# A spectral layer with routed experts: the cast of Y behind the next X on ScalarE, the gate products behind bias and first-stage copy on VectorE

## The chip, the core and the metric

One core of a Trainium2 chip runs the kernel. The metric is device time in microseconds of one execution. TensorE (PE) does the matmuls, VectorE (DVE) and ScalarE (ACT) empty PSUM and do elementwise work, POOL (GpSimd) does elementwise work on SBUF only and two indirect DMAs per expert batch, SyncE (SP) issues the other DMAs.

## The reference

Eight sequences of 3136 rows and 256 columns go through a Fourier layer and then through one expert that takes 128 rows of each:

```python
X = np.fft.rfft(x, axis=1)
Yr = Xr @ w_r - Xi @ w_i + b_r
Yi = Xr @ w_i + Xi @ w_r + b_i
Y = sign(Y) * np.maximum(np.abs(Y) - 0.01, 0)      # both parts
x = np.fft.irfft(Y, n=3136, axis=1)
scores = np.einsum('bsd,d->bs', x, w_gate)
top = the 128 rows of the largest scores of each sequence
out[b, top] = x[b, top] + sigmoid(scores[b, top]) * (relu(x[b, top] @ w1) @ w2)
```

## The kernel before

3136 is 49 times 64, so the transform runs in two stages of matmuls with tables. `s1` is the first stage (49 points); it writes A to DRAM. `s2` reads A back (tile `av`), multiplies by the table `g_sb` into the PSUM tile `px`, and makes X. `spectral` multiplies X by the two weight matrices into `py`. `shrink_a` and `shrink_b` add the bias and apply the soft threshold, which gives Y. `s2i` and `s1i` are the inverse stages: `s2i` makes C (PSUM tile `s`, copied to `ct`, stored to DRAM), `s1i` reads C back (`cv`) and writes the output.

Products are exact to fp32 by pairs: each operand is a rounded part (`Xh`, `Yh`) and the rest (`Xl`, `Yl`), and `mm3` (L200 to L203) issues three matmuls for one. The elementwise work of a step is this. For X: ScalarE casts px to Xh (L429) and a negated half of it (L430), VectorE subtracts for the rest Xl (L431), POOL negates a part of Xl (L432). For Y: VectorE adds the bias in PSUM (L453), ScalarE makes r (L455), VectorE makes yf (L460), ScalarE casts yf to Yh (L462), POOL subtracts for Yl (L463). For C: ScalarE copies it to `ct` (L481), VectorE multiplies it by the gate vector and sums, in two instructions `junk` with a short read of the sum after each (L484): the gate pair.

Work is cut into steps of one group g (13 to a sequence; 12 of two slices and one, g = 12, of one slice) for 8 sequences, 104 steps. Step t issues, in this order: loads and stores; `s2` of step t+1; the first half of `spectral` of t; `s2i` of t-2 with its gate pair; the second half of `spectral`; `shrink_a` of t; `s1` of a sequence 20 steps ahead (8 in 13 steps), whose result ScalarE and VectorE copy by halves (L406, L407); `shrink_b` of t; `s1i` of a unit 32 steps back (8 in 13 steps), whose result ScalarE copies twice (`ot`, L518). Between these, `threads` advance the routing (scores, a search for the threshold by bits, positions; small VectorE operations and small matmuls into the PSUM tile `m`) and the expert's products.

From step 8 on `ordered` chains what these functions issue, so that PE, ScalarE, VectorE and SP keep the order in which the code issues it; POOL's order, and the place of what is not chained (routing, constants such as the casts `w2h` of the W2 slices, L193), is left to a scheduler. `px` has one PSUM buffer, `py` two, `s` four, `m` one; X and yf have two buffers each, Y three, r one.

Of the kernel before, what the change touches and what calls it, by code (L numbers as in the profile page):

```python
# [10 lines left out]
F32 = mybir.dt.float32  # L11
# [6 lines left out]
ALU = mybir.AluOpType  # L18

B, S, D = 8, 3136, 256  # L20
# [76 lines left out]
def fourier_moe(ctx: ExitStack, tc: tile.TileContext, x, w_r, w_i, b_r, b_i, wg, w1, w2,  # L97
                t_wf, t_wq, t_g, t_gi, t_m, t_dig, outs, cap):
    nc = tc.nc
# [3 lines left out]
    pool = ctx.enter_context(tc.tile_pool(name="work", bufs=2))  # L103
# [5 lines left out]
    As, Cs, xt, ct, av, cv, ot, X, Y, Csc, py, r1 = [{} for _ in range(12)]  # L109

    def c_tile(shape, dt, name):
        return const.tile(shape, dt, name=name)
# [13 lines left out]
    wgb = c_tile([128, D], F32, "wgb")  # L126
# [69 lines left out]
    def pair(h_shape, tag, bufs):  # L196
        return (pool.tile(h_shape, F32R, name=tag + "h", bufs=bufs),
                pool.tile(h_shape, F32R, name=tag + "l", bufs=bufs))

    def mm3(out, wh, wl, mh, ml, start=True, stop=True):  # L200
        nc.tensor.matmul(out, wh, mh, start=start, stop=False)  # L201
        nc.tensor.matmul(out, wl, mh, start=False, stop=False)  # L202
        return nc.tensor.matmul(out, wh, ml, start=False, stop=stop).ins  # L203
# [167 lines left out]
    def width(g):  # L371
        return 1 if g == G - 1 else 2
# [3 lines left out]
    def store(dst, src):  # L376
        if t < 0:
            nc.sync.dma_start(out=dst, in_=src)
        else:
            stores.append((dst, src))  # L380
# [76 lines left out]
    def shrink_b(b, g):  # L457
        w = width(g)
        yf = pool.tile([128, w, D], F32, name="yf")
        nc.vector.scalar_tensor_tensor(out=yf, in0=py.pop((b, g)), scalar=0.0, in1=r1.pop((b, g)), op0=ALU.min, op1=ALU.add)  # L460
        yh, yl = pair([128, w, D], "Y", YB)
        nc.scalar.copy(out=yh, in_=yf)  # L462
        nc.gpsimd.tensor_tensor(out=yl, in0=yf, in1=yh.bitcast(F32), op=ALU.subtract)  # L463
        Y[b, g] = yh, yl

    def s2i(b, g):
        w = width(g)
        if g == 0:
            Cs[b] = As[b]
            Csc[b] = pool.tile([128, NJ], F32, name="Csc")  # L470
            nc.vector.memset(Csc[b][:, NJ - 1:], 0.0)
        if g % 2 == 0:
            ct[b] = pool.tile([128, 4, D], F32, name="ct")
        yh, yl = Y.pop((b, g))
        r = 128 if w == 2 else 64
        p = ps.tile([r, w, D], F32, name="s", bufs=4)
        for q in range(w):
            main_pe[0] = mm3(p[:, q, :], gih[:, 2 * g + q, :r], gil[:, 2 * g + q, :r], yh[:, q, :], yl[:, q, :])
        o = 2 * (g % 2)
        c = ct[b][:r, o:o + w, :]  # L480
        nc.scalar.copy(out=c, in_=p)  # L481
        for k in range(w):
            junk = pool.tile([128, D], F32, name="junk", bufs=1)
            nc.vector.tensor_tensor_reduce(out=junk[:r], in0=c[:, k, :], in1=wgb[:r], scale=1.0, scalar=0.0,  # L484
                                           op0=ALU.mult, op1=ALU.add, accum_out=Csc[b][:r, 2 * g + k:2 * g + k + 1])
        if w == 1:
            store(Cs[b][:, N1 - 1].rearrange("h n d -> n h d"), ct[b][:r, o, :].rearrange("p (h d) -> p h d", h=2))
        elif g % 2 == 1:
            for h in range(2):
                store(Cs[b][h, 4 * g - 4:4 * g + 4].rearrange("(j q) n d -> (q n) j d", q=2), ct[b][:, :, 128 * h:128 * h + 128])  # L490

    def score(b):
        p = ps.tile([NJ, 128], F32, name="m", bufs=1)
# [28 lines left out]
    G, U, ORD = 13, 8, 8  # L522
# [54 lines left out]
    def tick(ts):  # L577
        for g in list(ts):
            if g is urgent:
                with tc.high_priority():  # L580
                    end = next(g, 0) == 0
            else:
                end = next(g, 0) == 0
            if end:
                ts.remove(g)
# [3 lines left out]
    def ordered(f, *args, engines=()):  # L589
        bb = nc.cur_bb.bb.instructions  # L590
        n = len(bb)
        f(*args)
        for i in bb[n:]:
            if i.engine in (engines or (PE, ACT, DVE, SP)):
                if i.engine in chain:
                    tc.add_manual_dep(i, chain[i.engine].name, mybir.DependencyInfo(
                        mybir.DependencyClass.NoSync, mybir.DependencyReason.DATA), reason="main order")
                chain[i.engine] = i

    def at_step(u, f, n, kind=None):  # L600
        if 0 <= u < B * G:
            for i in range(-(-(u * n) // G), -(-((u + 1) * n) // G)):
                if t < ORD:
                    f(*divmod(i, n))
                else:
                    ordered(f, *divmod(i, n))
                if kind and i % n == n - 1:
                    done[kind] = i // n
# [19 lines left out]
    for t in range(-LEAD, B * G):  # L628
        if t + LEAD < G:
            at_step(t + LEAD, s1, U)  # L630
        if t == -2:
            consts_g(1)
            consts_gi(0)
        at_step(t + AP, ld_a, G)
        for i in range(U):
            if t == -3 + i * 8 // U:
                ld_x(1, i)
        if t + LEAD + XP >= 2 * G:
            at_step(t + LEAD + XP, ld_x, U)
        to_step(t + 2, ld_c)  # L640
        if t < ORD:
            flush()
        else:
            ordered(flush)
        if t % 2 == 0 and (t + 4) // 2 in range(2, 7):
            consts_g((t + 4) // 2)
        if t % 2 and (t + 1) // 2 in range(0, 6):
            consts_gi((t + 1) // 2 + 1)
        if t == 10:
            consts_b()  # L650
        if t in range(20, 20 + 2 * (FF // 128 + 2), 2):
            consts_moe((t - 20) // 2)
        at_step(t + 1, s2, G)
        tick(threads)
        at_step(t, lambda b, g: spectral(b, g, 0), G)
        if t == B * G - 1:
            at_step(t, shrink_a, G)
            at_step(t, shrink_b, G)
        at_step(t - 2, s2i, G, "s2i")
        if t == B * G - 1:  # L660
            break
        at_step(t, lambda b, g: spectral(b, g, 1), G)
        at_step(t, shrink_a, G)
        for i in range(U):
            if t == i * 8 // U:
                s1(1, i)
        if t + LEAD >= 2 * G:
            at_step(t + LEAD, s1, U)
        at_step(t, shrink_b, G)
        if t < B * G - 2:  # L670
            to_step(t, s1i)
        tick(threads)
        if main_pe[0] is not None:
            with tc.issue_after(main_pe[0]):
                ticks[0] += 1
                tick(ffns)
# [27 lines left out]
    unit()  # L704
    fill(0)
    unit()
    ordered(s2i, B - 1, G - 2)
    ordered(s2i, B - 1, G - 1)
    done["s2i"] = B - 1
    ordered(flush)  # L710
    stored = True
# [41 lines left out]
```

## Time and profile before

| | |
|---|---|
| median of 3 runs | 741.06 us (740.42 to 743.32) |
| the profiled execution | 740.18 us, its span 738.4 us |
| PE busy | 685.0 us, 93% of the span |
| weight loads busy | 556.9 us, 75% |
| VectorE busy | 455.2 us, 62% |
| ScalarE busy | 378.6 us, 51% |
| POOL busy | 223.8 us, 30% |
| DMA moved | 195.29 MB, mean 264 GB/s |
| share of the last chain | PE 46%, VectorE 21%, ScalarE 13%, DMA 9% |

Busy is the time in which an engine has an instruction under way. The ends of matmuls are modelled: a matmul is listed as longer than the distance to the next. An idle time is shown with what ended it. All groups of rows below come from the profiled execution.

### The profile page before, as it was taken

What the parts mean: (1) busy time and instruction counts of PE and PEld (TensorE: products, weight loads), DVE (VectorE), ACT (ScalarE), POOL (GpSimd) and SP (SyncE); (2) the same over time, 40 slices, a digit from 0 to 9 for tenths busy, and PEclk for the clock granted to TensorE, in tenths of its full rate; (3) what the DMA queues carried; (4) which work ended last, traced back from release to release, by engine and by line L of the source; (5) the groups of instructions that cost most, each with busy time, mean ns of one, the idle gap of its engine ahead of it and who ended that gap; (6) DMA issues with size and microseconds to landing.
All of it is one profiled execution on the core that took longest, in us unless ns stands there. A gap on an engine that the chain in (4) does not pass through costs nothing.

```text
span 738.4 us, 15016 instructions
## 1 busy us (share of the span) xinstructions
PE 685.0 (93%) x5482; PEld 556.9 (75%) x5482; DVE 455.2 (62%) x1330; ACT 378.6 (51%) x759; POOL 223.8 (30%) x255
## 2 busy tenths in 40 slices
PE   6299999999999999999999999999899999988997
PEld 2188787988877778887888787777778887865666
DVE  3146566565545555555677667777786758876752
ACT  3045545555555555656555655555555445445441
POOL 0043333233333332223233333322322322223221
PEclk9589999999999999999999999999999999999999
DMA  8888987787888899989999998897567765656961
GB/s 318 307 287 287 342 273 217 240 260 221 249 282 273 271 320 323 304 293 340 320 301 300 329 302 279 306 305 257 192 200 230 237 190 172 215 175 212 363 245 40
DMA packets 146407, 195.29 MB, mean 264 GB/s; under 512 B 8453, under 2 KB 111262, under 8 KB 146334
## 3 DMA queue, kind: packets, MB, share of 16 engines
q1 hardware_dynamic: 145278, 192.10, 78.3%
q0 software_dynamic: 912, 2.21, 0.9%
q8 instruction: 43, 0.70, 0.4%
q14 instruction: 30, 0.25, 0.1%
q10 hardware_dynamic: 144, 0.03, 0.0%
HBM read 100.58 MB, written 93.85 MB: 263 GB/s over the span
## 4 chain that ended last, share of the span: by engine, by line
PE 46%; DVE 21%; ACT 13%; DMA 9%; issue 8%; SPq 1%; POOL 1%; DVEq 0%; POOLq 0%; ACTq 0%
PE s L391 10%; PE px L426 7%; PE py L201 6%; PE py L203 6%; PE py L202 6%; DVE yf L460 4%; DVE junk L484 4%; ACT r L455 4%; DVE py L453 4%; ACT ot L518 3%; DVE Xl L431 3%; DMA xe<-in_moe_w 3%; ACT Xh L429 2%; PE s L203 2%; PE s L201 2%
## 5 line engine op out<-in xcount | busy, mean ns | idle before, releaser
L463 POOL TENSOR_TENSOR Yl<-yf,Yh 128x512 fp32r<-128x512 f32 (+1 forms) x104 | 133.5, 1284 | 314.5 <-ACT Yh L462 314.5
L455 ACT ACTIVATE r<-py,m2l 128x512 f32<-128x512 f32 (+1 forms) x104 | 69.9, 672 | 192.8 <-DVE py L453 178.3
L431 DVE TENSOR_TENSOR Xl<-px,Xh 128x512 fp32r<-128x512 f32 (+1 forms) x104 | 69.7, 670 | 150.3 <-ACT Xh L430 128.3
L426 PEld LDWEIGHTS px<-g_sb,av 128*128 128x128 f32 (+1 forms) x800 | 99.2, 194 | 67.0 <-DVE Csc L484 18.7
L426 PE MATMUL px<-g_sb,av 128*128 128x128 f32 (+1 forms) x800 | 117.6, 289 | 25.0 <-DMA av<-As 14.6
L201 PE MATMUL py<-wrh,Xh 128*128 128x256 f32 x400 | 122.8, 307 | 0.0
L202 PE MATMUL py<-wrh,Xl 128*128 128x256 f32 x400 | 112.9, 282 | 0.0
L203 PE MATMUL py<-wrl,Xh 128*128 128x256 f32 x400 | 112.8, 282 | 0.0
L201 PE MATMUL py<-wih,Xh 128*128 128x256 f32 x400 | 112.7, 282 | 0.0
L202 PE MATMUL py<-wih,Xl 128*128 128x256 f32 x400 | 112.2, 281 | 0.0
L203 PE MATMUL py<-wil,Xh 128*128 128x256 f32 x400 | 112.2, 280 | 0.0
L460 DVE SCALAR_TENSOR_TENSOR yf<-py,r 128x512 f32<-128x512 f32 (+1 forms) x104 | 69.7, 670 | 51.0 <-ACT r L455 50.0
L484 DVE CUSTOM_DVE_ANT_0 junk<-ct,wgb 128x256 f32<-128x256 f32 (+1 forms) x200 | 92.0, 460 | 14.1 <-ACT ct L481 10.8
L462 ACT CAST Yh<-yf 128x512 fp32r<-128x512 f32 (+1 forms) x104 | 62.8, 603 | 57.3 <-DVE yf L460 56.9
L432 POOL TENSOR_SCALAR Xl<-Xl 128x256 fp32r<-128x256 f32 (+1 forms) x104 | 50.2, 482 | 113.7 <-DVE Xl L431 86.8
L201 PEld LDWEIGHTS py<-wrh,Xh 128*128 128x128 f32 x400 | 76.5, 191 | 2.7 <-issue 1.4
L391 PE MATMUL s<-xt,w1f 49*64 49x512 f32 x480 | 70.6, 646 | 6.7 <-DMA w1f<-t_wf 5.0
L202 PEld LDWEIGHTS py<-wrh,Xl 128*128 128x128 f32 x400 | 76.5, 191 | 0.0
L203 PEld LDWEIGHTS py<-wil,Xh 128*128 128x128 f32 x400 | 75.6, 189 | 1.1 <-issue 1.1
L203 PEld LDWEIGHTS py<-wrl,Xh 128*128 128x128 f32 x400 | 76.2, 190 | 0.0
L201 PEld LDWEIGHTS py<-wih,Xh 128*128 128x128 f32 x400 | 75.8, 190 | 0.3 <-issue 0.3
L202 PEld LDWEIGHTS py<-wih,Xl 128*128 128x128 f32 x400 | 75.6, 189 | 0.2 <-POOL Xl L432 0.2
(125 smaller groups left out, 1210.7 us busy)
## 6 DMA issues: line engine op xcount, KB each, us to landing
xt<-in_x SPq DMA_DIRECT2D x60, 512.0 KB, 5.1
As<-at SPq DMA_DIRECT2D x59, 512.0 KB, 4.0
cv<-As SPq DMA_DIRECT2D x58, 512.0 KB, 5.6
out<-ot SPq DMA_DIRECT2D x57, 512.0 KB, 3.1
av<-As SPq DMA_DIRECT2D x96, 256.0 KB, 5.1
As<-ct SPq DMA_DIRECT2D x96, 256.0 KB, 4.5
out<-at SPq DMA_DIRECT2D x7, 512.0 KB, 2.7
xt<-As SPq DMA_DIRECT2D x6, 512.0 KB, 10.2
```

The costliest lines, as they stand in the source:

```text
L201: nc.tensor.matmul(out, wh, mh, start=start, stop=False)
L202: nc.tensor.matmul(out, wl, mh, start=False, stop=False)
L203: return nc.tensor.matmul(out, wh, ml, start=False, stop=stop).ins
L391: last_mm = nc.tensor.matmul(out[r][64 * c:64 * c + 64], w[64 * r:64 * r + N1, :], src(r, c), start=True, stop=True)
L426: nc.tensor.matmul(px[:, 2 * p + h, :], a[:, h, 2 * (g % 2) * (w - 1) + p, :], g_sb[:r, 2 * g + p, :], start=True, stop=True)
L431: nc.vector.tensor_tensor(out=xl[:, :, NF:], in0=px, in1=xh[:, :, NF:].bitcast(F32), op=ALU.subtract)
L432: nc.gpsimd.tensor_scalar(out=xl[:, :, :NF], in0=xl[:, :, 2 * NF:].bitcast(F32), scalar1=-1.0, scalar2=1.0, op0=ALU.mult, op1=ALU.mult)
L455: nc.scalar.activation(out=r1[b, g], in_=p, func=AF.Relu, bias=m2l, scale=1.0)
L460: nc.vector.scalar_tensor_tensor(out=yf, in0=py.pop((b, g)), scalar=0.0, in1=r1.pop((b, g)), op0=ALU.min, op1=ALU.add)
L462: nc.scalar.copy(out=yh, in_=yf)
L463: nc.gpsimd.tensor_tensor(out=yl, in0=yf, in1=yh.bitcast(F32), op=ALU.subtract)
L484: nc.vector.tensor_tensor_reduce(out=junk[:r], in0=c[:, k, :], in1=wgb[:r], scale=1.0, scalar=0.0, op0=ALU.mult, op1=ALU.add, accum_out=Cs ...
```

## The change

`shrink_b` is cut in two. What makes yf stays; the cast to Yh and POOL's subtraction become `shrink_c`, issued a step later, behind `s2` of the next step. The gate pair leaves `s2i` and becomes `gate`, issued behind `shrink_a` and `s1` and ahead of `shrink_b`.

```diff
--- before.py
+++ after.py
@@ -458,6 +458,11 @@
         w = width(g)
         yf = pool.tile([128, w, D], F32, name="yf")
         nc.vector.scalar_tensor_tensor(out=yf, in0=py.pop((b, g)), scalar=0.0, in1=r1.pop((b, g)), op0=ALU.min, op1=ALU.add)
+        Y[b, g] = yf
+
+    def shrink_c(b, g):
+        w = width(g)
+        yf = Y[b, g]
         yh, yl = pair([128, w, D], "Y", YB)
         nc.scalar.copy(out=yh, in_=yf)
         nc.gpsimd.tensor_tensor(out=yl, in0=yf, in1=yh.bitcast(F32), op=ALU.subtract)
@@ -479,15 +484,20 @@
         o = 2 * (g % 2)
         c = ct[b][:r, o:o + w, :]
         nc.scalar.copy(out=c, in_=p)
-        for k in range(w):
-            junk = pool.tile([128, D], F32, name="junk", bufs=1)
-            nc.vector.tensor_tensor_reduce(out=junk[:r], in0=c[:, k, :], in1=wgb[:r], scale=1.0, scalar=0.0,
-                                           op0=ALU.mult, op1=ALU.add, accum_out=Csc[b][:r, 2 * g + k:2 * g + k + 1])
         if w == 1:
             store(Cs[b][:, N1 - 1].rearrange("h n d -> n h d"), ct[b][:r, o, :].rearrange("p (h d) -> p h d", h=2))
         elif g % 2 == 1:
             for h in range(2):
                 store(Cs[b][h, 4 * g - 4:4 * g + 4].rearrange("(j q) n d -> (q n) j d", q=2), ct[b][:, :, 128 * h:128 * h + 128])
+
+    def gate(b, g):
+        w = width(g)
+        r = 128 if w == 2 else 64
+        c = ct[b][:r, 2 * (g % 2):2 * (g % 2) + w, :]
+        for k in range(w):
+            junk = pool.tile([128, D], F32, name="junk", bufs=1)
+            nc.vector.tensor_tensor_reduce(out=junk[:r], in0=c[:, k, :], in1=wgb[:r], scale=1.0, scalar=0.0,
+                                           op0=ALU.mult, op1=ALU.add, accum_out=Csc[b][:r, 2 * g + k:2 * g + k + 1])
 
     def score(b):
         p = ps.tile([NJ, 128], F32, name="m", bufs=1)
@@ -651,13 +661,16 @@
         if t in range(20, 20 + 2 * (FF // 128 + 2), 2):
             consts_moe((t - 20) // 2)
         at_step(t + 1, s2, G)
+        at_step(t - 1, shrink_c, G)
         tick(threads)
         at_step(t, lambda b, g: spectral(b, g, 0), G)
         if t == B * G - 1:
             at_step(t, shrink_a, G)
             at_step(t, shrink_b, G)
-        at_step(t - 2, s2i, G, "s2i")
+            at_step(t, shrink_c, G)
+        at_step(t - 2, s2i, G)
         if t == B * G - 1:
+            at_step(t - 2, gate, G, "s2i")
             break
         at_step(t, lambda b, g: spectral(b, g, 1), G)
         at_step(t, shrink_a, G)
@@ -666,6 +679,7 @@
                 s1(1, i)
         if t + LEAD >= 2 * G:
             at_step(t + LEAD, s1, U)
+        at_step(t - 2, gate, G, "s2i")
         at_step(t, shrink_b, G)
         if t < B * G - 2:
             to_step(t, s1i)
@@ -704,8 +718,9 @@
     unit()
     fill(0)
     unit()
-    ordered(s2i, B - 1, G - 2)
-    ordered(s2i, B - 1, G - 1)
+    for g in (G - 2, G - 1):
+        ordered(s2i, B - 1, g)
+        ordered(gate, B - 1, g)
     done["s2i"] = B - 1
     ordered(flush)
     stored = True
```

What this does to the order is seen on ScalarE around the last cast of a W2 slice (`w2h`). A row is a source line, an operation, what it writes and reads, and its size. Before:

```order
L455 ACTIVATE r_2974<-py,m2l 128x256
L193 CAST w2h<-xe 128x256
L406 COPY at<-s 128x512
L462 CAST Yh<-yf 128x256
L518 COPY ot<-s 128x4x128 x2
L429 CAST Xh<-px 128x4x128
L430 ACTIVATE Xh<-px 128x4x64
L481 COPY ct<-s 128x512
L455 ACTIVATE r_3055<-py,m2l 128x512
L462 CAST Yh<-yf 128x512
L429 CAST Xh<-px 128x4x128
```

After:

```order
L455 ACTIVATE r_2970<-py,m2l 128x256
L406 COPY at<-s 128x512
L193 CAST w2h<-xe 128x256
L528 COPY ot<-s 128x4x128 x2
L429 CAST Xh<-px 128x4x128
L430 ACTIVATE Xh<-px 128x4x64
L467 CAST Yh<-yf 128x256
L486 COPY ct<-s 128x512
L455 ACTIVATE r_3051<-py,m2l 128x512
L429 CAST Xh<-px 128x4x128
L430 ACTIVATE Xh<-px 128x4x64
```

The cast of Y stood ahead of the output copies and of both casts of X; it stands behind them, ahead of the copy of C. The first-stage copy (`at`) has changed places with the W2 cast.

On VectorE, a step of one slice in the first sequence with the step ahead of it. Before:

```order
L431 TENSOR_TENSOR Xl<-px,Xh 128x4x128
L484 ISA junk,Csc<-ct,wgb 128x256
L484 ISA Csc 128x1
L484 ISA junk,Csc<-ct,wgb 128x256
L484 ISA Csc 128x1
L453 TENSOR_TENSOR py<-py,bias 128x256
L407 COPY at<-s 128x512
L460 SCALAR_TENSOR_TENSOR yf<-py,r_1142 128x256
L431 TENSOR_TENSOR Xl<-px,Xh 128x4x128
```

After:

```order
L431 TENSOR_TENSOR Xl<-px,Xh 128x4x128
L453 TENSOR_TENSOR py<-py,bias 128x256
L407 COPY at<-s 128x512
L499 ISA junk,Csc<-ct,wgb 128x256
L499 ISA Csc 128x1
L499 ISA junk,Csc<-ct,wgb 128x256
L499 ISA Csc 128x1
L460 SCALAR_TENSOR_TENSOR yf<-py,r_1138 128x256
L431 TENSOR_TENSOR Xl<-px,Xh 128x4x128
```

The four instructions of the gate pair stood between Xl and the bias; they stand behind the bias and the first-stage copy and ahead of yf.

On POOL, in the steps that follow, with the numbers of the tiles (counted in the order in which the program makes them). Before:

```order
L463 TENSOR_TENSOR Yl_1038<-yf_1035,Yh_1037 128x512
L432 TENSOR_SCALAR Xl_1048<-Xl_1048 128x2x64
L463 TENSOR_TENSOR Yl_1096<-yf_1093,Yh_1095 128x512
L432 TENSOR_SCALAR Xl_1110<-Xl_1110 128x4x64
L463 TENSOR_TENSOR Yl_1156<-yf_1153,Yh_1155 128x256
L432 TENSOR_SCALAR Xl_1168<-Xl_1168 128x4x64
```

After:

```order
L432 TENSOR_SCALAR Xl_1044<-Xl_1044 128x2x64
L468 TENSOR_TENSOR Yl_1050<-yf_1035,Yh_1049 128x512
L468 TENSOR_TENSOR Yl_1112<-yf_1093,Yh_1111 128x512
L432 TENSOR_SCALAR Xl_1106<-Xl_1106 128x4x64
L468 TENSOR_TENSOR Yl_1170<-yf_1153,Yh_1169 128x256
L432 TENSOR_SCALAR Xl_1164<-Xl_1164 128x4x64
```

In the narrow step (the row of 128x2x64) Yl and the negation have changed places; otherwise Yl stays ahead of the negation of a part of Xl. In the new program this Xl is the older tile of the two: it is made first and negated second.

## Rows read from the trace of the kernel before

**Rows 1.** The page of the profile: busy us, share of the span, instructions.

```profile
PE 685.0 (93%) x5482; PEld 556.9 (75%) x5482; DVE 455.2 (62%) x1330; ACT 378.6 (51%) x759; POOL 223.8 (30%) x255
```

**Rows 2.** Table of stretches of 100 us: busy us of each engine (instructions), clock, DMA share, GB/s.

```profile
100.00:200.00 100.00, 96.59 (x800) 84.05 (x799) 60.52 (x149) 54.40 (x112) 34.92 (x41) 1.00 0.76 236
300.00:400.00 100.00, 99.90 (x829) 81.54 (x825) 61.89 (x158) 59.72 (x120) 30.19 (x34) 1.00 0.93 311
```

**Rows 3.** PE's waits: what waited, for whom, us in total, times, longest.

```profile
PE px L426 <- DVE Xl L431: 9.6, 11, 1.6
```

**Rows 4.** The same table for the weight loads.

```profile
PEld px L426 <- DVE Xl L431: 16.8, 18, 2.2
```

**Rows 5.** Timeline, 108 to 114 us, PE, VectorE, ScalarE, POOL: start, duration, [idle before].

```profile
108.28 1.16 PE L426 MATMUL px<-g_sb,av 128*128 128x128 f32 x8
113.84 1.16 PE L426 MATMUL px<-g_sb,av 128*128 128x128 f32 x8 [1.29 <-DVE Xl L431]
...
108.22 0.70 DVE L484 CUSTOM_DVE_ANT_0 junk<-ct,wgb 128x256 f32<-128x256 f32 x1
109.31 0.69 DVE L453 TENSOR_TENSOR py<-py,bias 128x512 f32<-128x512 f32 x1
110.89 0.69 DVE L460 SCALAR_TENSOR_TENSOR yf<-py,r 128x512 f32<-128x512 f32 x1 [0.89 <-ACT r L455]
113.09 0.69 DVE L431 TENSOR_TENSOR Xl<-px,Xh 128x512 fp32r<-128x512 f32 x1 [1.51 <-ACT Xh L430]
...
110.10 0.69 ACT L455 ACTIVATE r<-py,m2l 128x512 f32<-128x512 f32 x1 [1.91 <-DVE py L453]
111.61 0.62 ACT L462 CAST Yh<-yf 128x512 fp32r<-128x512 f32 x1 [0.83 <-DVE yf L460]
112.14 0.58 ACT L429 CAST Xh<-px 128x512 fp32r<-128x512 f32 x1
...
112.31 1.27 POOL L463 TENSOR_TENSOR Yl<-yf,Yh 128x512 fp32r<-128x512 f32 x1 [3.24 <-ACT Yh L462]
113.87 0.51 POOL L432 TENSOR_SCALAR Xl<-Xl 128x256 fp32r<-128x256 f32 x1 [0.29 <-DVE Xl L431]
```

**Rows 6.** Timeline around two casts of W2 slices, ScalarE and PE.

```profile
183.60 0.41 ACT L193 CAST w2h<-xe 128x256 fp32r<-128x256 f32 x1 [2.44 <-DMA xe<-in_moe_w]
...
181.51 1.16 PE L426 MATMUL px<-g_sb,av 128*128 128x128 f32 x8 [1.27 <-DVE Xl L431]
186.96 1.16 PE L426 MATMUL px<-g_sb,av 128*128 128x128 f32 x8 [0.75 <-DVE Xl L431]
...
261.19 0.41 ACT L193 CAST w2h<-xe 128x256 fp32r<-128x256 f32 x1 [1.46 <-DMA xe<-in_moe_w]
261.50 0.58 ACT L406 COPY at<-s 128x512 f32<-128x512 f32 x1
262.28 1.08 ACT L518 COPY ot<-s 128x512 f32<-128x512 f32 x2
...
264.97 1.16 PE L426 MATMUL px<-g_sb,av 128*128 128x128 f32 x8 [1.58 <-DVE Xl L431]
```

**Rows 7.** Timeline, PE, three matmuls in a row at 311 us.

```profile
310.97 0.28 PE L202 MATMUL py<-wih,Xl 128*128 128x256 f32 x1
311.09 0.27 PE L203 MATMUL py<-wil,Xh 128*128 128x256 f32 x1
311.47 1.16 PE L426 MATMUL px<-g_sb,av 128*128 128x128 f32 x8
```

**Rows 8.** Timeline at 92 us, VectorE and POOL.

```profile
92.11 1.29 DVE L484 CUSTOM_DVE_ANT_0 junk<-ct,wgb 128x256 f32<-128x256 f32 x1 [0.73 <-ACT ct L481]
...
91.83 1.29 POOL L171 TENSOR_TENSOR gip<-gi,gip 128x512 fp32r<-128x512 f32 x1
```

**Rows 9.** Timeline, PE, first and last wait for the routing's small results.

```profile
504.65 0.43 PE L501 MATMUL m<-sct,wq 25*64 25x32 f32 x8 [0.57 <-DVE d L258]
...
667.26 0.63 PE L306 MATMUL m<-row,hot 128*128 128x34 f32 x4 [0.71 <-DVE row L292]
```

## Prediction, written before the changed kernel was run

> **What bounds the kernel now.** I read the busy table first: TensorE (PE) is busy for 685.0 of 738.4 us [rows 1]. The table by stretches says where the rest lies: between 300 and 400 us PE is busy for 99.9 of 100 us, between 100 and 200 us for 96.6, at full granted clock in both [rows 2]. So in the middle the only thing to be won is what PE waits for. The table of waits names it: eleven times, 9.6 us together, the first matmul on a group of A (px, L426) waited for VectorE's rest of X (Xl, L431), because px has one PSUM buffer and Xl is its last reader [rows 3]. The weight loads show the same wait 18 times, 16.8 us [rows 4].
>
> The timeline of one such step shows why Xl is late [rows 5]. px starts at 108.28 and takes 1.16, so X could be cast from 109.44. But VectorE first runs the gate pair of an older C (108.22 to 109.31), then the bias (109.31), which ScalarE's r follows at 110.10, yf at 110.89, the cast of Y at 111.61, and only then the cast of X at 112.14; Xl starts at 113.09 and the next px at 113.84, 1.29 late. The chain is gate, bias, r, yf, Yh, Xh, Xl. Two of its links have nothing to do with X: the gate pair and Yh.
>
> **The change part by part.** No instruction is added or dropped; ScalarE, VectorE and POOL do the same work.
>
> *Gate behind bias and first-stage copy.* The pair leaves the stretch before the bias. In the step of [rows 5] the bias can then start when its last spectral matmul ends, about 108.4 (px followed at 108.28), not 109.31. r comes 0.79 later, as now, at 109.2, and is done about 0.65 later. The pair, at 1.09 us [rows 5], runs while r runs, 109.0 to 110.1; yf follows, 110.1 to 110.7. So yf comes 0.8 earlier. Cover: where a first-stage copy stands between too, r is hidden by that copy already and yf moves up less, by about 0.3; those steps also have some 1 us more of PE work.
>
> *Y's cast behind X.* Xh now waits only for r and its own px: 109.85 instead of 112.14. From Xh to Xl is 0.95 and from Xl to the next px 0.75 [rows 5]: Xl at 110.8, px possible at 111.55. PE itself is ready at 113.84 - 1.29 = 112.55. So 1.0 us of cover is left, and the wait goes. What is late next is PE itself.
>
> *What is put off.* Yh goes from 111.61 to about 110.8 here (its yf came earlier); in steps with output copies, where it used to precede two copies and Xh, it gets some 1.5 us later. POOL's rest of Y follows it 0.70 later and takes 1.27 [rows 5]; s2i wants it only a whole step on, behind the next px and half a spectral product. At zero, for that. The gate's sums are wanted once per sequence, after its last step. SP's order differs in one place only, the load of a W2 slice against a store of C; at zero. PE's order differs only in where the small matmuls of the routing stand.
>
> *The sum.* What PE really lost is more than the 9.6. The recorded end of a matmul lies 0.27 behind its start while the next starts 0.12 later [rows 7], so a wait of up to 0.15 shows no idle time and a longer one looks 0.15 too short: 311.09 to 311.47 is 0.38, of which 0.26 is lost, and 0.11 of it at most is recorded as idle. With 18 waits of the weight loads: 9.6 + 18 x 0.16 = 12.5. Bounds: 9.6 from [rows 3], 16.8 from [rows 4] (a weight load's wait also counts time in which earlier matmuls still run). I take 12.5, nearer the matmuls' own rows.
>
> Not all of it goes. At 183.60 and at 261.19 ScalarE waited 2.44 and 1.46 us for a W2 slice from DMA, in front of the casts [rows 6]. At the second, the order after has the first-stage copy ahead of that cast and Y's cast behind X, so the 0.78 from 261.50 to 262.28 goes of the wait of 1.58 at 264.97; 0.8 stays. At the first, Xh follows the slice directly, without r, a copy and Y's cast between; but PE arrives earlier by the 1.27 won at 181.51. The wait of 0.75 at 186.96 could go or more than stay; I let 0.7 stay. Together 1.5.
>
> 12.5 - 1.5 = 11.0 us. The profiled execution took 740.2 us (1.8 outside its span): 729.2. The median of the runs shown is 0.9 higher, so I forecast **730.0 us**. The routing stretch, 504 to 668 us, I leave unchanged: PE waits there 15 times, 11.2 us in all, for small VectorE results, the first and the last in [rows 9]. The pair now stands between bias and yf, where VectorE idles 0.89 for r in steps without a copy [rows 5]; that hides nearly all of it. But the small operations are reordered, which may give or take 3 us.
>
> *A port.* At 92.11 a gate product took 1.29 us beside a POOL operation that ran from 91.83 to 93.12, and ended 0.28 after it [rows 8]; in [rows 5] the whole pair takes 1.09. So it stood still. POOL's Yl is moved here, so what it meets counts. From the times above it runs 111.5 to 112.8 and the next pair starts, behind the next bias, after 113: they miss each other by little. By the rows the sum stays. The Trainium skill, SBUF — State Buffer, section Who interferes with whom, says that a VectorE instruction with two SBUF inputs and a POOL instruction that reads SBUF exclude each other, the loser standing fully still; [rows 8] agree for the VectorE side, and that POOL stands still too no row here shows. By that rule the sum would be the same where they miss and is the third rival where they meet.
>
> **The rivals.**
> *Late weights* (chance 0.09). If ScalarE's waits for the W2 slices do not move up as PE does, they swallow what is won between 175 and 265 us: seven waits, the first and the last in [rows 6], 6.0 us, and 0.16 each hidden, 1.1. Left are 12.5 - 7.1 = 5.4: 734.8, as median 735.7. For it: the two casts of [rows 6], DMA 0.93 busy from 300 to 400 us [rows 2]. Against: these loads are issued behind stores of C and A which also come earlier.
>
> *The waits change owner* (0.07). Xl now stands behind the pair and yf. If the pair takes 1.0 longer than 1.09 the cover of 1.0 is gone and Xl is as late as PE's own work allows or later; with as much again the old waits are back: 740. Against: from 111.55 to 112.55 there is room.
>
> *The rest of X pays* (0.06, slower). POOL runs Yl ahead of the quarter of Xl that it negates (L432), and Yl now starts behind X's cast. In the step of [rows 5]: Yh 110.8, Yl 111.5 to 112.8, the negation to 113.3 (0.51). Half a spectral product needs it at 112.55 + 1.1 + 6 x 0.12 = 114.35; the cover is 1.05 us. If Yl and the negation slide by more than that, every one of 104 steps pays: at 0.11 us a step the gain is used up, at 0.2 it is 20.8 - 11.0 = 9.8 slower, 751. For it: the port, which the pair and POOL share; against: the pair, about 1.09 long [rows 5], lies behind a bias that waits for PE, when POOL is done.
>
> That the change does not do what it says is excluded by the order of instructions: Yh stands behind both casts of X, the pair behind the bias, from the eighth step to the last.
>
> **How the numbers follow.** My forecast has 0.78; its own range is 725.5 to 733.5, from 16.8 in place of 12.5 at one end, or 3 us of routing either way. Late weights lie above that, so the range goes to 738; the owner's and the slower case, 0.13, are left out. 0.5% (3.7 us, about what a measurement of this kernel can tell from no change) puts the borders at 737.4 and 744.8. Faster: 0.78 and 0.09, less a little, 0.86; same 0.08; slower 0.06.
>
> **What would show it.** In the profile after, ScalarE should cast X right after r (and the copies that precede it) with no stop for yf, and PE's waits for Xl should fall from 9.6 to about 1.5 us, those left near the W2 slices; PE's busy time stays near 685; VectorE's bias starts with the end of a spectral product in the short steps, and Xl ends at least 0.5 us ahead of the next px. I am wrong if waits of spectral matmuls (L202, L203) for POOL's part of Xl appear, if the routing's 11.2 us grow by more than 3, or if the waits for Xl are gone and the span is not shorter by some 10 us.

## The result: 716.9 us, and the profile after

The changed kernel takes **716.92 us** (median of 4 runs, 714.71 to 720.31) against 742.19 us of the kernel before in the same session (4 runs, 740.42 to 744.11): a ratio of 0.967, 95% interval 0.9638 to 0.9701. It is faster, by 25 us; the forecast was faster by 11, and the range (725.5 to 738) ended above it. The profiled execution after took 720.31 us with a span of 718.5, 19.9 us under the 738.4 of before. It is the slowest of its four, for a reason that the second half of this section shows.

The busy row of the page, and two stretches of 100 us, with the columns of [rows 1] and [rows 2]:

```profile
PE 678.8 (94%) x5482; PEld 556.6 (77%) x5482; DVE 467.2 (65%) x1330; ACT 383.5 (53%) x759; POOL 210.1 (29%) x255
```

```profile
100.00:200.00 100.00, 99.79 (x833) 87.58 (x832) 61.95 (x154) 57.94 (x116) 33.73 (x44) 1.00 0.81 253
300.00:400.00 100.00, 100.00 (x846) 83.45 (x845) 68.06 (x174) 61.94 (x124) 29.54 (x37) 1.00 0.95 320
```

PE has nearly the work of before, 678.8 for 685.0 us. Between 100 and 200 us it is now busy for 99.8 of 100 us, before for 96.6. Where it stood still has shrunk. PE's waits and then the weight loads' waits (what waited, for whom, us in total, times, longest), the rows that answer to [rows 3] and [rows 4]:

```profile
PE px L426 <- DVE Xl L431: 1.0, 2, 0.8
```

```profile
PEld px L426 <- DVE Xl L431: 3.0, 3, 1.6
PEld s L391 <- ACT ct L486: 2.8, 3, 1.6
```

The waits of px for the rest of X fell from 9.6 to 1.0 us. The forecast was about 1.5, left near the W2 slices; of the 1.0, 0.8 lies at 89.9 us, ahead of the first slice, so the size was met by luck. The last row is one whose counterpart I had not weighed. In the same table of the kernel before it reads:

```profile
PEld s L391 <- ACT ct L481: 9.0, 18, 1.7
```

The first stage (s, L391) needs a PSUM buffer that ScalarE's copy of C (ct) must free, and that copy stands behind Xh in ScalarE's order. So what made X late made ct late.

The step that the prediction worked through (108.28 to 113.84 in [rows 5]) now looks like this, in the timeline of PE, VectorE and ScalarE (start, duration, engine, [idle before]):

```profile
105.42 1.05 PE L426 MATMUL px<-g_sb,av 128*128 128x128 f32 x8
105.62 0.70 DVE L453 TENSOR_TENSOR py<-py,bias 128x512 f32<-128x512 f32 x1 [1.94 <-PE py L203]
...
106.23 0.41 DVE L499 CUSTOM_DVE_ANT_0 junk<-ct,wgb 128x256 f32<-128x256 f32 x1
...
106.42 0.69 ACT L455 ACTIVATE r<-py,m2l 128x512 f32<-128x512 f32 x1 [1.63 <-DVE py L453]
...
107.00 0.58 ACT L429 CAST Xh<-px 128x512 fp32r<-128x512 f32 x1
...
107.21 0.69 DVE L460 SCALAR_TENSOR_TENSOR yf<-py,r 128x512 f32<-128x512 f32 x1
...
107.93 0.62 ACT L467 CAST Yh<-yf 128x512 fp32r<-128x512 f32 x1
107.95 0.69 DVE L431 TENSOR_TENSOR Xl<-px,Xh 128x512 fp32r<-128x512 f32 x1
...
108.62 0.58 ACT L486 COPY ct<-s 128x512 f32<-128x512 f32 x1
...
109.53 1.16 PE L426 MATMUL px<-g_sb,av 128*128 128x128 f32 x8
```

From px to px it is 109.53 - 105.42 = 4.11 us, for 5.56 before. The links went as worked out: ScalarE casts X at 107.00, straight behind r, and Yh waits for yf and stands behind; the pair runs beside r; the rest of X ends at 108.64, 0.9 us ahead of px.

To see where the 19.9 us came from I paired the matmuls of the two traces one by one and compared, pair by pair, the distance from one start to the next. That also counts what is hidden in overlapping ends. Gains, in us, of the kernel after on the kernel before:

| stretch (times of before) | at px (L426) | at s (L391) | elsewhere | sum |
|---|---|---|---|---|
| 0 to 38 | -1.1 | 2.4 | 0 | 1.3 |
| 38 to 503, without 245 to 251 | 14.2 | 5.2 | 0.3 | 19.7 |
| 245 to 251 | -0.7 | -2.1 | -2.4 | -5.2 |
| 503 to 668, routing | 0.9 | 0 | 2.5 | 3.4 |
| 668 to the end | 0 | 0.7 | 0.1 | 0.8 |

So from 38 to 503 us the waits of px were worth 14.2 and the first stage's waits for ct 5.2; the routing gave 3.4, and at one place 5.2 was lost. The 1.3 at the start belongs to this execution: in the profiles of after_again and w2_later below it is -0.5. The place of the loss lies at 234 to 246 us in the time of the kernel after. The timeline of ScalarE and of PE, and the table by stretches, show:

```profile
234.82 0.40 ACT L193 CAST w2h<-xe 128x256 fp32r<-128x256 f32 x1 [4.00 <-DMA xe<-in_moe_w]
```

```profile
238.02 1.42 PE L391 MATMUL s<-cv,w1tf 49*64 49x512 f32 x4 [0.69 <-ACT ct L486]
```

```profile
235.00:239.00 4.00, 3.31 (x17) 0.78 (x16) 1.94 (x4) 3.51 (x8) 2.17 (x3) 0.95 0.50 166
239.00:246.00 7.00, 7.00 (x33) 6.41 (x32) 1.94 (x6) 3.23 (x8) 1.73 (x3) 0.54 0.97 311
246.00:252.00 6.00, 6.00 (x53) 4.63 (x52) 4.59 (x12) 4.41 (x10) 2.06 (x3) 1.00 0.99 321
```

ScalarE stood 4.00 us in front of a W2 slice that had not landed; ct behind it came late; PE stood still for 0.69 us at s; and from 239 to 246 us, PE being busy all the time, the granted clock is 0.54 in the mean. From the means of the stretches it was 0.50 (1.2 GHz) from about 238.6 to 245.4. The rows count 33 matmuls in these 7.00 us and 53 in the 6.00 us behind them. Without this loss the profiled execution would have taken some 715 us, which is where two of the other three runs lie.

### The profile page after: what moved, and what is told of

The parts are those of the page before. It is cut to its first block, busy times and chain, and to the rows that moved or that the text cites. A ratio compares the mean times of both kernels' runs of the same rounds, so it can differ in the third digit from the quotient of the medians.

```text
span 718.5 us, 15022 instructions
## 1 busy us (share of the span) xinstructions
PE 678.8 (94%) x5482; PEld 556.6 (77%) x5482; DVE 467.2 (65%) x1330; ACT 383.5 (53%) x759; POOL 210.1 (29%) x255
## 4 chain that ended last, share of the span: by engine, by line
PE 78%; DVE 10%; DMA 5%; issue 3%; ACT 2%; SPq 1%; POOL 0%; POOLq 0%; DVEq 0%; ACTq 0%
PE s L391 16%; PE py L201 12%; PE px L426 12%; PE py L203 11%; PE py L202 11%; PE s L201 3%; PE s L203 3%; PE s L202 3%; PE py L345 2%; DMA As<-ot 1%; DVE junk L499 1%; DVE yf L460 1%; PE s L345 1%; DVE py L453 1%; DVE Xl L431 1%
## 5 line engine op out<-in xcount | busy, mean ns | idle before, releaser
L468 POOL TENSOR_TENSOR Yl<-yf,Yh 128x512 fp32r<-128x512 f32 (+1 forms) x104 | 130.4, 1254 | 349.1 <-ACT Yh L467 349.0
L426 PEld LDWEIGHTS px<-g_sb,av 128*128 128x128 f32 (+1 forms) x800 | 99.7, 194 | 54.6 <-DVE py L453 17.9
L453 DVE TENSOR_TENSOR py<-py,bias 128x512 f32<-128x512 f32 (+1 forms) x104 | 70.3, 676 | 99.3 <-PE py L203 95.8
L426 PE MATMUL px<-g_sb,av 128*128 128x128 f32 (+1 forms) x800 | 116.1, 287 | 16.2 <-DMA av<-As 15.2
L499 DVE CUSTOM_DVE_ANT_0 junk<-ct,wgb 128x256 f32<-128x256 f32 (+1 forms) x200 | 87.3, 437 | 9.2 <-ACT ct L486 6.0
L486 ACT COPY ct<-s 128x512 f32<-128x512 f32 (+1 forms) x104 | 59.3, 572 | 54.8 <-PE s L203 53.5
L391 PE MATMUL s<-xt,w1f 49*64 49x512 f32 x480 | 71.3, 646 | 5.5 <-DMA w1f<-t_wf 5.1
L429 ACT CAST Xh<-px 128x512 fp32r<-128x512 f32 (+1 forms) x104 | 59.5, 572 | 31.7 <-PE px L426 24.7
```

The costliest lines, as they stand in the source:

```text
L391: last_mm = nc.tensor.matmul(out[r][64 * c:64 * c + 64], w[64 * r:64 * r + N1, :], src(r, c), start=True, stop=True)
L426: nc.tensor.matmul(px[:, 2 * p + h, :], a[:, h, 2 * (g % 2) * (w - 1) + p, :], g_sb[:r, 2 * g + p, :], start=True, stop=True)
L429: nc.scalar.copy(out=xh[:, :, NF:], in_=px)
L453: nc.vector.tensor_tensor(out=p, in0=p, in1=bias[:, :w, :], op=ALU.add)
```

## The experiments

Each was timed on one chip together with the kernel before. "Ratio" is to that, with its 95% interval. Edits are against the kernel after unless the kernel before is named, and "..." marks lines left out. The table also has the length of the two shortest steps of the kernel after, number 14 (the one of the prediction) and number 27, from px to px in the timeline:

| kernel | step 14 | step 27 | median us | ratio |
|---|---|---|---|---|
| before | 5.56 | 5.55 | 742 | 1 |
| y_only | 5.05 | 5.32 | 738.45 | 0.9955 (0.9936 to 0.9973) |
| gate_only | 4.73 | 4.73 | 731.11 | 0.9855 (0.9829 to 0.9881) |
| y_ct | 4.11 | 4.11 | 725.53 | 0.9773 (0.9725 to 0.982) |
| after_again | 4.11 | 4.10 | 716.83 | 0.9666 (0.9636 to 0.9695) |
| after_ct | 4.11 | 4.11 | 718.27 | 0.9662 (0.9613 to 0.9711) |
| pair_twice | 4.11 | 4.24 | 726.69 | 0.9786 (0.9738 to 0.9835) |
| before_twice | 6.48 | 6.48 | 814.92 | 1.0974 (1.0933 to 1.1015) |
| px_two | 5.72 | 5.70 | 742.23 | 1.0006 (0.9978 to 1.0034) |
| w2_later | 4.11 | 4.11 | 715.81 | 0.9645 (0.9619 to 0.967) |
| w2_ct | 4.11 | 4.11 | 712.89 | 0.9633 (0.96 to 0.9665) |
| warm | 4.11 | 4.10 | 716.79 | 0.9677 (0.9652 to 0.9701) |
| warm13 | 4.11 | 4.11 | 712.19 | 0.9599 (0.9565 to 0.9634) |

For after_again, y_only, gate_only and w2_later my theory was still the chain of the prediction, with ct behind it.

**after_again**, the changed kernel, nothing edited.

> The changed kernel once more, as a measure for the others. Theory (a late W2 slice makes ScalarE stand 4.00 us at 234.8, PE then stands still for 0.69 us and runs at 1.2 GHz from 239.4 to 246.3): where the slice lands in time the time is 715 us, where it lands late 718 to 720; the five runs spread over some 5 us. Rival (the fall of the clock has another cause in the program's order): all runs near 717, the profile with the clock at 0.50 after 239 us again.

716.83 us (715.24 to 719.99, 6 runs). The runs spread over 4.8 us as expected, and in the profile of this one, of 717 us, the clock stands at 1.00 from 200 to 300 us. So the fall of the clock is not fixed in the program; it comes in some executions.

**y_only**, Y's cast alone.

```diff
         at_step(t - 2, s2i, G)
+        at_step(t - 2, gate, G, "s2i")
...
-        at_step(t - 2, gate, G, "s2i")
         at_step(t, shrink_b, G)
```

> Only the cast of Y goes behind X; the gate pair stays ahead of the bias. Theory (one chain, gate, bias, r, yf, Yh, Xh, Xl, makes X late and, behind X on ScalarE, the copy of C that frees the buffers of the first stage): Xh now waits for r alone, in the step at 112 us 1.4 us earlier than before, about as much as PE lost there; most of the gain comes: 722 us (718 to 727). Rival (the gate pair on VectorE is what counts, by freeing the first-stage copy L407 and the bias): 735 to 740.

738.45 us, where 722 was expected: a clear miss, the gain is a seventh of what both parts bring. Two rows of the page, the gate products in the kernel after and here, and the timeline at 106 us show why:

```profile
L499 DVE CUSTOM_DVE_ANT_0 junk<-ct,wgb 128x256 f32<-128x256 f32 (+1 forms) x200 | 87.3, 437 | 9.2 <-ACT ct L486 6.0
```

```profile
L499 DVE CUSTOM_DVE_ANT_0 junk<-ct,wgb 128x256 f32<-128x256 f32 (+1 forms) x200 | 136.4, 682 | 34.0 <-ACT ct L486 30.2
```

```profile
105.97 0.58 ACT L486 COPY ct<-s 128x512 f32<-128x512 f32 x1
...
106.40 1.27 POOL L468 TENSOR_TENSOR Yl<-yf,Yh 128x512 fp32r<-128x512 f32 x1
106.58 1.37 DVE L499 CUSTOM_DVE_ANT_0 junk<-ct,wgb 128x256 f32<-128x256 f32 x1 [0.53 <-ACT ct L486]
...
108.35 0.69 DVE L453 TENSOR_TENSOR py<-py,bias 128x512 f32<-128x512 f32 x1
...
111.79 1.11 DVE L499 CUSTOM_DVE_ANT_0 junk<-ct,wgb 128x256 f32<-128x256 f32 x1 [0.42 <-ACT ct L486]
```

In the first two rows the columns are line, engine, operation, tiles, count, then busy us and mean ns, then idle us before. The copy of C now stands behind Y's cast, which waits for yf; the pair waits for the copy, 30.2 us in all instead of 6.0; and it comes just when POOL has begun the rest of Y. The first product then takes 1.37 us instead of 0.42 and ends 0.28 behind POOL's operation. 66 of the 200 products took over 0.7 us, in the kernel after 4. What Y's cast gives on ScalarE, the bias pays back on VectorE: from pair to pair this turn is 111.79 - 106.58 = 5.21 us, 0.95 of it the time that the first product stood still. Without that, 4.26 would be left, little over the 4.11 of the same step in the kernel after.

**gate_only**, the pair alone.

```diff
-        at_step(t - 1, shrink_c, G)
...
         at_step(t, shrink_b, G)
+        at_step(t, shrink_c, G)
```

> Only the gate pair moves behind bias and first-stage copy; the cast of Y stays ahead of X. Theory (one chain): yf, Yh and Xh come 0.8 us earlier than before, which covers the waits of up to 0.8 us and shortens those of 1.2 to 1.6: 730 us (726 to 735), with 2 to 4 us of waits of px for Xl left. Rival (the pair is what counts): 717 to 722. Second rival (the pair alone brings nothing since r is waited for anyway): 740.

731.11 us, where 730 was expected, with 5.3 us of waits of px for Xl left, somewhat more than the 2 to 4 expected. The parts alone give 3.6 and 10.9 us, both in one kernel 25. Waits that add up one by one would not do that; y_only's new stops beside POOL are part of the difference.

**The theory then.** The chain closes on itself. Before, pair, bias, r, yf, Yh, Xh, Xl and ct are one loop: the next pair stands behind Xl in VectorE's order and needs ct, both of which wait for Xh, and Xh stands behind Yh, which waits for yf, which waits for the pair. In [rows 5] a turn goes from the pair at 108.22 to the next one, which stands in the same timeline at 113.70:

```profile
113.70 0.41 DVE L484 CUSTOM_DVE_ANT_0 junk<-ct,wgb 128x256 f32<-128x256 f32 x1
```

That is 5.48 us, and the step takes 5.56. In such a step VectorE and ScalarE cannot turn faster, whatever PE does. A step with more work of PE than that builds up room ahead of px, which a shorter one behind it may use up; where none is left, PE goes at the loop's pace, and lateness is handed on from turn to turn. By the orders of the instructions, Y's cast alone leaves a loop pair, bias, r, Xh, Yh, ct, pair; the gate's move alone leaves bias, r, yf, Yh, Xh, Xl, bias; both together leave only bias, r, Xh, Xl. The rival was px's single buffer, which the prediction had named.

**y_ct**: like y_only, with Y's cast also behind the copy of C. That takes Yh out of the loop that was left, and it also lets the pair start ahead of POOL's rest of Y.

```diff
-        at_step(t - 1, shrink_c, G)
+        if t == B * G - 1:
+            at_step(t - 1, shrink_c, G)
...
         at_step(t - 2, s2i, G)
+        if t < B * G - 1:
+            at_step(t - 1, shrink_c, G)
+        at_step(t - 2, gate, G, "s2i")
...
-        at_step(t - 2, gate, G, "s2i")
         at_step(t, shrink_b, G)
```

> Y's cast behind X and also behind the copy of C; the gate pair stays ahead of the bias. Theory (with only Y moved the pair waited for a copy of C behind Y's cast, and then stood still beside POOL's rest of Y: 66 of 200 products over 0.7 us, 136.4 us in all): now the copy of C is 0.53 us earlier and the rest of Y starts behind it, so the products are back at 0.42 to 0.47 each, under 95 us in all, and the time falls from 738 to 726 us (722 to 731). Rival (Y's cast is worth little as long as bias and r stand behind the pair): 736 to 740, with short products.

725.53 us, where 726 was expected. The products take 103.6 us, where under 95 was expected, and 21 of them over 0.7 us:

```profile
L499 DVE CUSTOM_DVE_ANT_0 junk<-ct,wgb 128x256 f32<-128x256 f32 (+1 forms) x200 | 103.6, 518 | 64.6 <-ACT ct L486 61.0
```

In the long middle the steps are those of the changed kernel (14 and 27 take 4.11; from step 13 to step 83, at 484 us in after_again, it loses 0.4 us on that run). So for the long middle it is enough that Y's cast stands behind the copy of C; the pair may stay ahead of the bias. Whether Yh's place in the loop or the pair's stops beside POOL made y_only slow is not parted by this: y_ct removes the one and most of the other, and in the step shown the stop is the larger. Ahead of step 13 y_ct falls 3.0 us behind after_again, 2.1 of them in one step in which PE waits 1.26 us for Yl. The pair's place counts in the routing stretch: against before, y_ct loses 0.2 us from 503 us to the end, while after_ct, which differs from it in the pair's place alone, wins 7.7 there. In y_ct VectorE stands 61.0 us in front of the pair, waiting for ct, and the routing's small operations queue behind it; that this is why that stretch is longer is argued from the order, not shown.

**after_ct**: the changed kernel with Y's cast behind the copy of C, as above, and the pair where the change puts it.

> The changed kernel with Y's cast also behind the copy of C. Theory (in the changed kernel the copy of C waits for PE, 53.5 us in 63 waits, so Y's cast ahead of it costs nothing; the rest of Y has about 1.4 us to spare behind it): as the changed kernel, 716 us (714 to 719). Rival (the first stage's wait for the copy of C is still the next bound): 713 or less. Second rival (the rest of Y comes too late for the inverse product): 720 or more, with PE waits for Yl.

718.27 us (715.77 to 719.08), where 716 (714 to 719) was expected: no difference from the changed kernel that this measurement can tell. PE waits 1.7 us for Yl, in three places, so there is less than the room I gave it; in this execution, too, the clock fell, between 232 and 233 us, behind a slice that ScalarE waited 2.71 us for.

**pair_twice and before_twice**: every gate product computed twice, in the kernel after and in the kernel before.

```diff
-        for k in range(w):
+        for k in [*range(w), *range(w)]:
             junk = pool.tile([128, D], F32, name="junk", bufs=1)
```

> The changed kernel with every gate product computed twice (the second time into the same places), some 1.0 us more VectorE work between bias and yf in each of 104 steps. Theory (the pair runs while ScalarE works on r, and the rest of X ends 1.67 us or more ahead of the next px in three quarters of the steps, under 1.0 us ahead in 9 of 73): only those few steps pay, and the routing's small operations a little: 721 us (718 to 727). Rival (the pair is on the way to X in most steps): 0.5 us and more a step, 760 or above.

> The kernel before with every gate product computed twice, as in pair_twice: some 1.0 us more VectorE work ahead of the bias in each step. Theory (before, a loop runs from step to step, pair, bias, r, yf, Yh, Xh, copy of C, next pair, 5.55 us long, and PE waits in every step whose own work is shorter): the two short steps at 112 and 180 us go from 5.55 to about 6.55 us, and by the room that the rest of X had ahead of px in the kernel before (under 1.0 us in 53 of 73 steps) the whole loses 37 us or more: 779 us (770 to 800). Rival (the pair costs no more ahead of the bias than behind it, and it was Y's cast alone that made X late): some 10 us as in pair_twice, 752.

The same work costs 10 us in the one (726.69, expected 721, within its range) and 73 in the other (814.92, expected 779 and at most 800: a miss). Of the 10 us, 1.7 lie between steps 13 and 83, on after_again, and 6.8 behind step 83; of the 73, 56.3 lie between the same steps. In before_twice steps 14 and 27 grew by 0.92 and 0.93 us; PE's waits for Xl there:

```profile
PE px L426 <- DVE Xl L431: 39.3, 35, 2.2
```

My 37 us counted each step's own room once; it came to twice that, which fits lateness that passes on from turn to turn: the mean step between 13 and 83 grew by 0.80 us. Some 9 of the 56.3 may be the clock's: from 107 to 563 us its mean there is 0.98, and 2% of 456 us is 9. That the pair lies in the loop before, and beside it after, is thereby shown.

**px_two**: the kernel before with two PSUM buffers for px (the tiles m share them).

```diff
-    BUFS = {"s": 4, "px": 1, "py": 2, "m": 1}
+    BUFS = {"s": 4, "px": 2, "py": 2}
...
-        px = ps.tile([128, 2 * w, 128], F32, name="px", bufs=1)
+        px = ps.tile([128, 2 * w, 128], F32, name="px", bufs=2)
```

> The kernel before with two PSUM buffers for px (the routing's small tiles m share them, instead of a buffer of their own); no order is changed. Theory (px's single buffer is what makes PE wait for the rest of X): up to 400 us PE's waits of px for Xl are gone and PE is 9 to 12 us ahead of the kernel before, against 11.5 of the changed kernel, while the first stage's weight loads still wait for the copy of C as before, 9 us; behind 400 us the sharing with the routing may take some of it: 731 us (727 to 738). Rival (PE then waits for X at the spectral product instead): 740 with new waits of L201 and L202.

742.23 us, no gain at all, where 731 was expected; the rival holds. PE's waits from 90 to 300 us, of this kernel and then of before:

```profile
PE py L202 <- DVE Xl L431: 3.2, 6, 0.7
PE s L391 <- ACT ct L481: 3.2, 3, 1.7
PE py L202 <- POOL Xl L432: 1.1, 1, 1.1
PE py L201 <- ACT Xh L429: 0.5, 1, 0.5
```

```profile
PE px L426 <- DVE Xl L431: 9.0, 10, 1.6
```

px no longer waits for Xl, and the 9.0 us turn up as 8.0 at the spectral product, which needs the same X, and at the first stage, which needs the same ct. Here the buffer moves the wait; the turn of the loop stays. The shared buffers do not hide a gain in that stretch: paired with before as in the table above, the matmuls from 38 to 503 us gain 15.6 us at px and lose 7.8 at s and 7.9 elsewhere. Outside it, 4.3 us are won ahead of 38 us and 3.5 lost in the routing, where px and the small tiles share their buffers, so that the total is zero partly by chance.

**w2_later**: the changed kernel with the casts of the W2 slices taken out of the scheduler's hands.

```diff
             ld(t, w2[128 * f:128 * f + 128])
-            nc.scalar.copy(out=w2h[:, f, :], in_=t)
+            slices.append((f, t))
...
+        if t in range(26, 26 + 2 * (FF // 128), 2):
+            ordered(cast_moe)
```

> The changed kernel with the casts of the W2 slices fixed in ScalarE's order behind the copy of C, six steps after their load is issued. Theory (late slices cost PE time, by ScalarE's stop and by the clock that falls after it): ScalarE's waits for the slices, 19.0 us in the changed kernel, go to under 1; no clock of 0.50 near 239 us; 714 to 715 us, the runs within 2 us of each other. Rival (these waits are hidden and the fall of the clock has another cause): as the changed kernel, 717.

715.81 us (714.53 to 717.33, 6 runs), where 714 to 715 was expected and runs within 2 us of each other. ScalarE's waits for slices, 19.0 us in the changed kernel's profile, are gone, and from 200 to 300 us PE is busy throughout at full clock:

```profile
200.00:300.00 100.00, 100.00 (x846) 84.06 (x845) 57.50 (x139) 64.08 (x128) 33.73 (x42) 1.00 0.97 324
```

The median gain of 1.0 us over after_again lies within the uncertainty. This profile, undisturbed, is 24.6 us shorter than that of before.

**w2_ct**: w2_later and after_ct in one.

> The changed kernel with both: the casts of the W2 slices fixed six steps behind their load, and Y's cast behind the copy of C. Theory (late slices cost PE time and clock between 220 and 265 us; with Y's cast behind the copy of C the routing stretch from 503 to 668 us gained 7.3 us over before, 3.4 in the changed kernel): 713.5 us (712 to 716), no waits for a slice over 0.2 us, no clock of 0.50 behind 50 us. Rival (the routing's gain is a chance of the order in which the small operations come and does not add up): 716 to 718.

712.89 us (711.24 to 717.58, 6 runs): the median expected. The runs spread as widely as before, so the slices are not the only source of the spread; in the profile the clock fell once more, against the expectation (0.57 in the mean from 652 to 656 us). It is the lowest of the versions that only move work, below both kernels; against the changed kernel the intervals of the ratios overlap, so its 4 us are likely, not settled.

**warm and warm13**: w2_ct with 24, and then 13, matmuls that nobody reads on PE ahead of the first px, where PE stands still for 14 us.

```diff
+        if t == -1:
+            p = ps.tile([64, 4, 128], F32, name="m", bufs=1)
+            for _ in range(24):
+                nc.tensor.matmul(p, w1f, warm[0][:, :4, :], start=True, stop=True)
         at_step(t + 1, s2, G)
```

> As w2_ct, and 24 matmuls that nobody reads on PE ahead of the first px, where PE stood still from 17 to 31 us. Theory (PE's standing still brings the granted clock to 0.50 at about 22 us, and it stays there until 41 us, well behind the first px at 31.4): with PE busy the clock stays at 1.00 and the steps from 31.4 to 41 us, some 10 us of matmuls at half speed, take about 4.5 us less: 709 us (707 to 712). Rival (the first steps wait for DMA and ScalarE anyway, or the added matmuls delay px): 713 to 716, as w2_ct.

> As warm, with 13 of the unread matmuls in place of 24. In warm the 24 took 0.87 us each, 20.81 us from 18.99 on, so that px began at 39.7 instead of 31.1; the clock stood at 1.00 all the same and PE caught up 3.6 us by 100 us. Theory (the clock falls when PE stands still and costs some 4 us behind the start): 13 end at about 30.2, px starts at 31.1 as in w2_ct, and the steps behind it win 3.5 to 4.5 us: 709 us (708 to 711). Rival (behind the start PE waits for DMA and ScalarE whatever its clock): 713.

warm took 716.79 us, where 709 was expected and 716 at most by the rival: the 24 lasted until 39.7 us, px began 8.7 us late, and of these PE won back 3.6 at full clock. warm13 took 712.19, as w2_ct, where 709 was expected: its 13 ended at 29.6, PE then waited 1.96 us for A to land, and the table by stretches has the clock at 0.54 from 31 to 42 us all the same, where w2_ct (the second two rows) has 0.52:

```profile
20.00:31.00 11.00, 9.61 (x23) 2.88 (x21) 0.00 (x0) 0.00 (x0) 0.00 (x0) 1.00 0.80 313
31.00:42.00 11.00, 8.86 (x32) 6.77 (x33) 1.38 (x2) 2.36 (x5) 2.07 (x3) 0.54 0.95 315
```

```profile
20.00:31.00 11.00, 0.00 (x0) 0.00 (x0) 0.00 (x0) 0.00 (x0) 0.00 (x0) 0.55 0.81 316
31.00:42.00 11.00, 10.52 (x40) 8.38 (x41) 1.38 (x2) 2.36 (x5) 2.08 (x3) 0.52 0.90 313
```

So the clock stayed up in warm, where PE was not let stand, and not in warm13. A gain at the start is not shown.

## Why the prediction was wrong, step by step

*What bounds the kernel.* Right as far as it went: PE, less what it waits for, and the chain gate, bias, r, yf, Yh, Xh, Xl. Wrong in "because px has one PSUM buffer": px_two gives it two and nothing is won. And the chain is a loop: it closes through the next pair.

*The two moves.* Right in their working, for the step worked through. Counted from the start of px, the forecast had Xh at 1.57 us, yf at 1.8 and Xl at 2.5; in the step shown above they stand at 1.58, 1.79 and 2.53. What was put off cost nothing: in the kernel after no row of PE's waits, and none of the weight loads', names Yh or Yl.

*The sum.* Here it failed. "What PE really lost" was taken to be px's waits, 12.5 us; they were 14.2, within the bounds of 9.6 to 16.8. But the same lateness held up a second customer, the first stage, through ct: 5.2 us from 38 to 503 us that the sum put at nothing, without a reason. The row that shows it stood in the table from which [rows 4] are taken, 9.0 us in 18 waits; I read the one row that my chain led to. The routing, left unchanged with 3 us either way, gave 3.4; which of its operations gave it is not shown.

*Not all of it goes, 1.5.* In this execution nearly all of it went: one wait of 0.16 us is left near the slices, and w2_later, without waits for slices, wins 14.4 at px in the same stretch. In after_again, behind a slice that ScalarE waited 3.10 us for, px waited 1.25 us: the mechanism is there, its size differs from execution to execution. What the slices cost in this one was the stop of 4.00 us and the fall of the clock behind it, 5.2 us.

*The sum once more*: 14.2 + 5.2 + 3.4 + 0.8 + 1.3 at the start + 0.3 = 25.2, less 5.2 in the profiled execution. The medians differ by 25.3; that this is so close to 25.2 is partly chance, since some of the runs behind the median have such a loss as well and the 1.3 is not in every profile. Forecast 11.0: it lacked the 5.2 at s, 3.4 of the routing, 1.7 at px, the 1.5 taken off for the slices and 2.4 in the small terms.

*The port.* The rule that the prediction drew from the Trainium skill (SBUF — State Buffer, Who interferes with whom) gave no part of the sum, and in the kernel after such stops cost next to nothing: the pair's products take 437 ns in the mean, 460 before. The trace of y_only agrees with that rule: with Y's cast moved alone the pair meets POOL's rest of Y, and the products take 136.4 us instead of 87.3. The gate's move thus also keeps the pair clear of POOL's rest of Y. One reading was off: the pair of 1.09 us in [rows 5] had itself stood still. Its first product, 0.70 us where one alone takes 0.42, ended 0.29 behind this operation:

```profile
107.34 1.29 POOL L463 TENSOR_TENSOR Yl<-yf,Yh 128x512 fp32r<-128x512 f32 x1 [3.20 <-ACT Yh L462]
```

*The rivals.* Late weights: a late slice did cost time in this execution, once, 5.2 us by the first stage and the clock, not as the loss between 175 and 265 us that was feared. The waits change owner: not after the change, but exactly that in px_two. The rest of X pays: no spectral product waited for POOL's part of Xl.

*The range.* It put its bounds around one term and left another term out. With a loop between two engines, the recorded waits of one consumer were only one of the places in which its length showed.

## What to carry to other kernels

When two engines hand work to each other in fixed orders, look for a closed loop first: add up one turn from the timeline and compare it with the step of the engine that should be the bound. Where that engine's own work is shorter than a turn and no room is left from the step before, cutting the loop gains the difference, whoever is recorded as waiting; here another buffer for one consumer only moved the wait. Take all rows of the waits table that name a product of the same engine behind the late one, and test a part of a change alone before calling it half of the gain: here parts that gave 3.6 and 10.9 gave 25 together.

## What the runs showed of the hardware

The granted clock fell to half behind two short stops of PE: 0.69 us of standing still at 237.3 us in the kernel after was followed by 0.50 from about 238.6 to 245.4, although PE worked all that time; 1.96 us at 29.6 us in warm13 by 0.50 from about 32 to 42. The stop is the smaller part of the price: 0.69 of the 5.2 us. That a stop of this length is enough is not shown: in the kernel before, px's waits of 1.27 us at 181.51 and 1.58 at 264.97 [rows 6] left the clock at 1.00.

A gate product on VectorE (two inputs in SBUF) that starts while POOL's rest of Y is under way stands still until that is done: in y_only there are 74 of them, and each ends 0.27 to 0.29 us behind POOL's operation. Sorted by the POOL operation beside them, the 200 products of y_only took 0.42 us in the median alone (50 of them), 0.49 beside the negation of a quarter of Xl (70), and 1.11 beside the rest of Y (74). Which of the two starts first decides: in y_ct 81 products started ahead of POOL's rest of Y and took 0.42 in the median, and POOL's operation then took 1.46 us, against 1.27 where it started first. The routing's small operations feel it as well: f (L216) takes 0.17 us alone, and in the trace of after_again 1.18 in the median of the 12 cases beside the rest of Y.
